# Turning more tiles on the matrix engine in a two-stage kernel's second half, with products two, three and four steps behind

## The chip, the cores and the metric

One core of a Trainium2 chip runs the whole program. Its engines work at the same time and wait for each other by semaphores: TensorE (PE in the profile, its weight loads PEld), VectorE (DVE), ScalarE (ACT), GpSimd (POOL), and SyncE (SP), which issues nearly all DMAs. Each engine takes its instructions strictly in the order in which the program lists them. The metric is the device time of one execution in microseconds (us); lower is better.

## The reference

An input of 8 x 3072 x 256 floats goes through three layers:

```
X  = rfft(x, axis=1);  Y = soft(X @ (w_r + i w_i) + b, 0.01)   # complex, soft-thresholded
x1 = irfft(Y)                                                # 24576 tokens of 256
logits = x1 @ phi                                            # 32 slots
d = softmax over tokens;  slot = d.T @ x1;  slot_out = relu(slot @ w1) @ w2   # per expert
c = softmax over slots;   x2 = c @ slot_out
h = x2 @ w_in                                                # 1024 wide
solu = h * softmax(h);  ln = (solu - mean) / sqrt(var + 1e-6) * g
out = ln @ w_out                                             # 24576 x 256
```

Only the last four lines concern the second half of the kernel. There `x2` is never formed: `slot_out @ w_in` is folded into one matrix `gst` of 128 x 1024, so that h comes from the 32 slot weights `c` of a token alone, and the mean is taken out of `w_out` beforehand (`gw`).

## The kernel before

The first half (`phase1`) computes the transform, the thresholded mix and the slot sums, batch by batch, and leaves the weights c in DRAM. A short middle part at the head of `phase2` (lines 858 to 933) computes the expert outputs, `gw` (the scaled and centred output weights as a rounded part `gw[:, :, 0]` and a remainder `gw[:, :, 1]`) and `gst`. The change touches this part lightly and the loop after it heavily.

The loop works on 192 tiles of 128 tokens (`NI`). What a tile goes through, with the helper's name:

- `hmat`: TensorE forms hps = -h (128 x 1024) from `ct` and `gst`, two matmuls into one of three PSUM buffers.
- `rowmax`: VectorE takes the row minimum of hps (the maximum of h); `expo`: ScalarE makes e = exp(h - max) and its row sum; `umul`: VectorE makes u = hps * e and its row sum. The hps buffer is free after `umul`.
- `blocks`: VectorE transposes u in 32 x 32 blocks (tile `tb`), and four DMAs gather the blocks into `t2`, which is u transposed.
- `uhi`: ScalarE (three quarters) and GpSimd (one quarter) round t2 into uh; `ulo`: GpSimd subtracts, ul = t2 - uh, in two halves of 512 columns.
- `prod`: TensorE multiplies by `gw` into `po2`: 16 matmuls of uh and then 8 of ul, of which the first four need the first half of ul and the last four the second.
- `vari`: ScalarE squares u and sums (`sq`); `rstd`: every fourth step, at step 3 modulo 4, GpSimd turns the sums of four tiles into scales, by four small instructions (tile `st`, lines 1138 to 1141); `outp`: ScalarE copies two products with their scales into `osb`; `store`: one DMA for four tiles.

A *turned* tile goes another way: `hmat` uses `gstn` (the same matrix in the natural column order), `turn` transposes u on TensorE by 8 matmuls into the tile's own hps buffer, ScalarE copies that out (`raw`), and GpSimd rounds and subtracts only half of it (`turned_parts`); its product has 4 fp32 matmuls with `gwf` (the unrounded weights) and 12 others. It has no `blocks` and no DMAs. Before, tiles 22, 30, 38, ... 182 are turned, 21 of them. The last two tiles (`direct`) also go through TensorE.

The order of the work is written out by hand in the loop's body, and each engine follows it. In step i (turn i of the loop) stand `hmat` of tile i+3, `rowmax` i+2, `umul` and `blocks` i+1, `vari` i, `expo` i+2, `uhi` and `ulo` i-2 with `rstd` between the two halves of `ulo`, and last `prod` i-4. Around a turned tile T, step T-1 ends with 16 matmuls of a product, the 8 transposes of tile T, and the 8 that are left; step T begins with 12 matmuls of the next product and then `hmat` of T+3, which waits for the copy of tile T's transposes, as it writes the same buffer. Every matmul has line 89 and every transpose line 92, since helpers record them.

## Time and profile before

| | us |
|---|---|
| median of three runs | 1342.22 (1339.57 to 1346.41) |
| the profiled execution, its own time | 1338.72 |
| its span, first to last instruction | 1336.8 |
| first `hmat` of the loop | 644.4 |
| busy over the span: PE, DVE, ACT, POOL | 1261.9, 1143.4, 982.2, 1013.6 |
| granted TensorE clock, mean | 0.982 |

The loop takes the second half of the span, from 644 on. In the profile a row of the timeline gives the start, the length, the engine, the source line, the operation, the output and input tiles, the shape, and in brackets how long the engine had stood idle before and what released it. A matmul's length there includes the pipeline's latency, so the cost of a group of matmuls is read from its start to the start of what follows. The granted clock is 1.00 at TensorE's full 2.4 GHz and 0.50 at the lower level of 1.2 GHz.

### The profile page before, as it was taken

The page shows a single profiled execution, that of the slowest core. Times are in us where ns is not written, and L with a number is a line of the kernel's source. Part 1 is how long each engine was busy: PE and PEld are TensorE (multiplying, and loading weights), DVE is VectorE, ACT ScalarE, POOL GpSimd, SP SyncE. Part 2 cuts the span into 40 slices and gives each one's busy share as a digit, 9 for nine tenths or more (in the row PEclk, how much of TensorE's full clock was granted, in tenths as well). Part 3 has the DMA queues.
Part 4 walks back from the last instruction along what each step waited for, and adds up shares of the span by engine and source line. Part 5 has one row for each costly group of instructions (what it writes and reads, how often), then busy time and mean ns, then how long its engine had stood idle before and what let it go on. Part 6 is the DMA issues. An engine that isn't in the chain of part 4 may idle for free.

```text
span 1336.8 us, 30801 instructions
## 1 busy us (share of the span) xinstructions
PE 1261.9 (94%) x10964; PEld 1110.8 (83%) x10964; DVE 1143.4 (86%) x1559; ACT 982.2 (73%) x1829; POOL 1013.6 (76%) x1115
## 2 busy tenths in 40 slices
PE   5989999999999999888599999999999999999998
PEld 2867878787878778864398999999999999999998
DVE  1858898887888988765798999999999999999993
ACT  3445556565555564443598999999999999999995
POOL 0869596867777675331299999998999989998896
PEclk8999999999999999998799999999999999999999
DMA  8987374655647283349477777777777777777763
GB/s 268 276 218 191 116 207 125 175 158 139 180 111 220 73 242 113 96 157 348 97 165 195 187 209 199 199 182 184 199 197 197 180 190 198 191 197 177 196 170 110
DMA packets 185961, 241.77 MB, mean 181 GB/s; under 512 B 21968, under 2 KB 145232, under 8 KB 185808
## 3 DMA queue, kind: packets, MB, share of 16 engines
q1 hardware_dynamic: 185472, 238.62, 66.3%
q8 instruction: 87, 1.43, 0.5%
q10 hardware_dynamic: 336, 1.18, 0.3%
q14 instruction: 66, 0.54, 0.1%
HBM read 92.00 MB, written 59.11 MB: 113 GB/s over the span
## 4 chain that ended last, share of the span: by engine, by line
PE 69%; POOL 10%; DVE 8%; DMA 5%; issue 4%; ACT 2%; SPq 1%; POOLq 0%; ACTq 0%; DVEq 0%
PE po L89 34%; PE pb L89 7%; PE pm L89 6%; PE hps L89 6%; PE xps L89 5%; PE s L89 4%; PE pa L89 3%; POOL ul L1094 3%; DMA xc<-in_x_dram 2%; PE sps L92 2%; POOL x L223 1%; POOL x L227 1%; PE hps L92 1%; POOL s L342 1%; DMA t<-tb 1%
## 5 line engine op out<-in xcount | busy, mean ns | idle before, releaser
L1094 POOL TENSOR_TENSOR ul<-t,uh 128x512 fp32r<-128x512 f32 x338 | 432.2, 1294 | 38.3 <-ACT uh L1080 38.1
L89 PEld LDWEIGHTS po<-gw,uh 128*128 128x128 f32 x2736 | 350.5, 190 | 14.0
L89 PE MATMUL po<-gw,uh 128*128 128x256 f32 x2736 | 356.8, 282 | 0.0
L984 DVE TENSOR_REDUCE st<-hps 128x1 f32<-128x1024 f32 x192 | 229.1, 1194 | 14.3 <-PE hps L89 14.3
L89 PE MATMUL po<-gw,ul 128*128 128x256 f32 x1620 | 230.4, 285 | 6.8 <-POOL ul L1094 6.6
L999 DVE SCALAR_TENSOR_TENSOR u<-hps,e 128x1024 f32<-128x1024 f32 x192 | 232.2, 1209 | 0.5 <-ACT e L991 0.5
L991 ACT ACTIVATE e<-hps,st 128x1024 f32<-128x1024 f32 x192 | 215.2, 1121 | 16.9 <-DVE st L984 16.9
L1104 ACT ACTIVATE sq<-u,st 128x1024 f32<-128x1024 f32 x192 | 222.9, 1161 | 0.2 <-DVE u L999 0.2
L1022 DVE STREAM_TRANSPOSE tb<-u 128x1024 f32<-128x1024 f32 x169 | 210.5, 1245 | 6.6 <-DMA t<-tb 0.7
L89 PEld LDWEIGHTS po<-gw,ul 128*128 128x128 f32 x1620 | 207.0, 189 | 9.3 <-POOL ul L1094 8.2
L342 POOL TENSOR_TENSOR s<-yb,s 128x512 f32<-128x512 f32 x95 | 124.4, 1309 | 112.3 <-DVE s L341 108.7
L89 PEld LDWEIGHTS xps<-d_sb,apt 128*128 128x128 f32 x768 | 95.1, 194 | 59.6 <-issue 35.6
L1080 ACT ACTIVATE uh<-t 128x768 fp32r<-128x768 f32 x169 | 143.4, 849 | 0.4 <-DMA t<-tb 0.4
L89 PE MATMUL xps<-d_sb,apt 128*128 128x128 f32 x768 | 111.2, 288 | 12.5 <-DMA apt<-ad 9.6
L89 PE MATMUL hps<-gst,ct 128*128 128x512 f32 x338 | 107.6, 401 | 14.3 <-DVE u L999 12.9
L250 ACT ACTIVATE asb<-s 128x1024 f32<-128x1024 f32 x56 | 57.3, 1024 | 85.4 <-PE s L89 74.2
L223 POOL TENSOR_TENSOR x<-xc 112x512 f32<-112x512 f32 x56 | 74.7, 1334 | 42.7 <-DMA xc<-in_x_dram 39.3
L307 POOL TENSOR_TENSOR sl<-xsum,sh 128x256 fp32r<-128x256 f32 x93 | 74.8, 804 | 35.4 <-ACT sh L306 35.1
L291 DVE TENSOR_TENSOR xsum<-xps,xi 128x256 f32<-128x256 f32 x96 | 39.7, 414 | 68.0 <-ACT xh L290 47.8
L1081 POOL CAST uh<-t 128x256 fp32r<-128x256 f32 x169 | 67.6, 400 | 39.1 <-DMA t<-tb 39.1
L1155 ACT ACTIVATE osb<-po,st 128x256 f32<-128x256 f32 x192 | 80.1, 475 | 11.4 <-PE po L89 11.4
L227 POOL TENSOR_TENSOR x<-xc 112x512 f32<-112x512 f32 x56 | 80.3, 1433 | 0.0
(204 smaller groups left out, 2354.8 us busy)
## 6 DMA issues: line engine op xcount, KB each, us to landing
t<-tb SPq DMA_DIRECT2D x676, 128.0 KB, 2.8
xc<-in_x_dram SPq DMA_DIRECT2D x128, 192.0 KB, 4.1
apt<-ad SPq DMA_DIRECT2D x96, 256.0 KB, 4.2
out_dram<-osb SPq DMA_DIRECT2D x47, 512.0 KB, 3.7
ad<-asb SPq DMA_DIRECT2D x112, 192.0 KB, 3.9
ct<-c_dram SPq DMA_DIRECT2D x96, 128.0 KB, 4.0
wt<-in_moe_w_dram SPq DMA_DIRECT2D x21, 512.0 KB, 9.5
ws<-in_moe_w_dram SPq DMA_DIRECT2D x22, 256.0 KB, 5.9
```

The lines of the kernel that those rows point to most:

```text
L89: PE.matmul(out=out, lhsT=lhsT, rhs=rhs, start=start, stop=stop)
L223: POOL.tensor_tensor(out=z[0:112, 0], in0=t[:, 0], in1=t[:, 1], op=ALU.add)
L227: POOL.tensor_tensor(out=z[0:112, 1], in0=t[:, 0], in1=t[:, 1], op=ALU.subtract)
L342: (DVE if last else POOL).tensor_tensor(out=s, in0=y, in1=s, op=ALU.subtract)
L984: DVE.tensor_reduce(out=st[:, 0, k:k + 1], in_=hps[i], op=ALU.min, axis=AX.X)
L991: ACT.activation(out=e, in_=hps[i], func=AF.Exp, bias=st[:, 0, k:k + 1], scale=-1.0, accum_out=st[:, 1, k:k + 1])
L999: DVE.scalar_tensor_tensor(out=u, in0=hps[i] if turned(i) else hps.pop(i), scalar=1.0, in1=et.pop(i), op0=ALU.mult, op1=ALU.mult, accum_ou ...
L1022: DVE.transpose(out=t, in_=ut[i])
L1080: ACT.activation(out=w[:, 0:HA], in_=v[:, 0:HA], func=AF.Copy)
L1094: POOL.tensor_tensor(out=ul[:, z, :].rearrange("p c (a j) -> p c a j", a=4), in0=v, in1=w.bitcast(F32), op=ALU.subtract)
L1104: ACT.activation(out=sq, in_=ut.pop(i), func=AF.Square, bias=st[:, 2, k:k + 1], scale=-float(DFF), accum_out=st[:, 3, k:k + 1])
L1155: ACT.activation(out=o[:, k], in_=pot.pop(i), func=AF.Copy, scale=stt[j][:, 4, k:k + 1])
```

## The change

In the loop, five more tiles are turned (6, 10, 14, 18 and 26), so that up to 30 it is every fourth one, 26 in all. `prod` runs L steps behind, 2 for steps below 64, 3 below 128, then 4; at steps 64 and 128 one step has no product. `uhi` and `ulo` take tile i-1 in steps up to 95, none in step 96, and tile i-2 from step 97. `outp` runs as soon as both products of a pair are L+2 steps old or more (by the counter `pair`), and a store follows two steps after. In the first steps 24 matmuls of `ones` on `ones` go to a spare PSUM buffer (`run_on`). In the middle part the centring of `wo`, the rounding and the remainder are done in two halves, the first of which leaves its result in `gwf`; `gstn` is copied as `gst` is made; three h1 buffers serve h1 and h1t.

```
--- before.py
+++ after.py
@@ -835,6 +835,8 @@
         gw = k_p.tile([128, 8, 2, D], F32R, name="gw")
         gw_h, gw_l = gw[:, :, 0, :], gw[:, :, 1, :]
         gst = k_p.tile([128, DFF], F32R, name="gst")
+        gstn = k_p.tile([128, DFF], F32R, name="gstn")
+        gwf = k_p.tile([128, 4, D], F32, name="gwf")
         cts = {}
 
 
@@ -862,8 +864,10 @@
         load_c(0, 0)
         load_ws(len(ws_todo))
         wo = gw_t["wo"]
-        DVE.tensor_tensor(out=wo, in0=wo, in1=gm.to_broadcast([128, 8, D]), op=ALU.subtract)
-        ACT.activation(out=gw_h, in_=wo, func=AF.Copy)
+        g_halves = ((slice(0, 4), gwf), (slice(4, 8), wo[:, 4:8]))
+        for z, o in g_halves:
+            DVE.tensor_tensor(out=o, in0=wo[:, z], in1=gm.to_broadcast([128, 4, D]), op=ALU.subtract)
+            ACT.activation(out=gw_h[:, z], in_=o, func=AF.Copy)
 
 
         so = t_p.tile([128, 2, D], F32, name="so")
@@ -880,14 +884,14 @@
                             dh == 0,
                             dh == 1,
                         )
-            h1 = t_p.tile([128, DFF], F32, name="h1", tag="h1", bufs=2)
+            h1 = t_p.tile([128, DFF], F32, name="h1", tag="h1", bufs=3)
             ACT.activation(out=h1[:, 0:512], in_=ph[0], func=AF.Relu)
             DVE.tensor_scalar(out=h1[:, 512:1024], in0=ph[1], scalar1=0.0, scalar2=None, op0=ALU.max)
             h1s[eh] = h1
         load_c(0, 1)
         load_c(0, 2)
         for eh in range(2):
-            h1t = t_p.tile([128, 8, 128], F32, name="h1t", tag="h1t", bufs=2)
+            h1t = t_p.tile([128, 8, 128], F32, name="h1t", tag="h1", bufs=3)
             for k in range(2):
                 pst = pt.tile([128, 4, 128], F32, name="pst", tag="pt")
                 for j in range(4):
@@ -897,7 +901,8 @@
                 else:
                     ACT.activation(out=h1t[:, 4 * k:4 * k + 4, :], in_=pst, func=AF.Copy)
             h1ts[eh] = h1t
-        DVE.tensor_tensor(out=gw_l, in0=wo, in1=gw_h.bitcast(F32), op=ALU.subtract)
+        for z, o in g_halves:
+            DVE.tensor_tensor(out=gw_l[:, z], in0=o, in1=gw_h[:, z].bitcast(F32), op=ALU.subtract)
 
         wi_h = g_p.tile([128, 2, DFF], F32R, name="wi_h", tag="wo")
         for dh in range(2):
@@ -931,15 +936,15 @@
             v = pg[fh].rearrange("p (c j b) -> p b c j", c=4, b=4)
             ACT.activation(out=o, in_=v, func=AF.Copy)
             DVE.tensor_tensor(out=o[64:128], in0=v[64:128], in1=o[64:128].bitcast(F32), op=ALU.subtract)
+            POOL.tensor_copy(
+                out=gstn[:, 512 * fh:512 * fh + 512].rearrange("p (c j b) -> p b c j", c=4, b=4), in_=o.bitcast(F32)
+            )
         p.close()
         pw.close()
 
         def right(name, bufs, **k):
             return p2.enter_context(tc.tile_pool(name=name, bufs=bufs, side="right", **k))
 
-        f_p = right("f_p", 1)
-        gwf = f_p.tile([128, 8, D], F32, name="gwf")
-        gstn = f_p.tile([128, DFF], F32R, name="gstn")
         e_p = right("e_p", 2)
         u_p = right("u_p", 4)
         o_p = right("o_p", 2)
@@ -1004,16 +1009,7 @@
             return i >= NI - 2
 
         def turned(i):
-            return i % 8 == 6 and 16 < i < NI - 2
-
-        def gst_order():
-            POOL.tensor_copy(out=gstn.rearrange("p (c j b) -> p b c j", c=8, b=4), in_=gst.rearrange("p (b c j) -> p b c j", b=4, c=8).bitcast(F32))
-
-
-
-        def gw_sum(n):
-            z = slice(2 * n, 2 * n + 2)
-            POOL.tensor_tensor(out=gwf[:, z], in0=gw[:, z, 0].bitcast(F32), in1=gw[:, z, 1].bitcast(F32), op=ALU.add)
+            return i >= 6 and i % (4 if i < 32 else 8) == 2 + 4 * (i >= 32) and i < NI - 2
 
         def blocks(i):
             if i >= NI or direct(i) or turned(i):
@@ -1157,7 +1153,7 @@
 
                 SP.dma_start(out=v[:, k, :], in_=o[:, k, :])
             elif k == 3:
-                o_todo[i + 2] = (v, o)
+                o_todo[i] = (v, o)
 
 
         def store(i):
@@ -1194,27 +1190,40 @@
         pieces(1)
         for i in range(3):
             hmat(i)
+        idle = po_p.tile([128, 128], F32, name="idle", tag="po2")
+
+        def run_on():
+            for _ in range(8):
+                mm(idle, ones, ones)
+
+        run_on()
         rowmax(0)
         expo(0)
         rowmax(1)
         expo(1)
         umul(0)
         blocks(0)
+        pair = 0
         for i in range(NI + 6):
             j, k = divmod(i, 4)
+            L = 2 if i < 64 else 3 if i < 128 else 4
             if turned(i):
-                prod(i - 4, 12)
+                prod(i - L, 12)
             hmat(i + 3)
+            if i < 2:
+                run_on()
             trans(i)
             rowmax(i + 2)
             umul(i + 1)
             blocks(i + 1)
-            store(i - 6)
+            for t in [t for t in o_todo if t + L + 4 <= i]:
+                store(t)
             late_c(i)
             last_c(i)
-            if i % 2 == 1:
-                outp(i - 7)
-                outp(i - 6)
+            if 2 * pair + 3 + L <= i:
+                outp(2 * pair)
+                outp(2 * pair + 1)
+                pair += 1
             if turned(i):
                 expo(i + 2)
                 vari(i)
@@ -1222,22 +1231,19 @@
                 vari(i)
                 expo(i + 2)
             direct_parts(i)
-            if i <= NI + 1:
-                uhi(i - 2)
-                ulo(i - 2, 0)
+            m = i - (1 if i < 96 else 2)
+            if i != 96 and 0 <= m < NI:
+                uhi(m)
+                ulo(m, 0)
             rstd(i)
-            if i <= NI + 1:
-                ulo(i - 2, 1)
-            if i == 8:
-                gst_order()
-            if i in (10, 12, 14, 16):
-                gw_sum(i // 2 - 5)
+            if i != 96 and 0 <= m < NI:
+                ulo(m, 1)
             if k == 1:
                 pieces(j + 2)
             if turned(i + 1):
-                prod(i - 4, 8)
+                prod(i - L, 8)
                 turn(i + 1)
-            prod(i - 4)
+            prod(i - L)
         while o_todo:
             store(min(o_todo))
 
```

The first place is TensorE's start of the loop, from the second hps on: hps are the `hmat` products, po2 the products of uh and ul. Before:

```order
L89 MATMUL hps_8654<-gst_8355,ct_8386 128x512 x2
L89 MATMUL hps_8671<-gst_8355,ct_8386 128x512 x2
L89 MATMUL hps_8695<-gst_8355,ct_8386 128x512 x2
L89 MATMUL hps_8722<-gst_8355,ct_8386 128x512 x2
L89 MATMUL po2_8745<-gw_8354,uh_8689 128x256 x16
L89 MATMUL po2_8745<-gw_8354,ul_8690 128x256 x8
L89 MATMUL hps_8770<-gst_8355,ct_8442 128x512 x2
L89 MATMUL po2_8745<-gw_8354,uh_8712 128x256 x16
L89 MATMUL po2_8745<-gw_8354,ul_8713 128x256 x8
```

And now:

```order
L89 MATMUL hps_8617<-gst_8355,ct_8388 128x512 x2
L89 MATMUL hps_8620<-gst_8355,ct_8388 128x512 x2
L89 MATMUL idle_8623<-ones_64 128x128 x8
L89 MATMUL hps_8648<-gst_8355,ct_8388 128x512 x2
L89 MATMUL idle_8623<-ones_64 128x128 x8
L89 MATMUL hps_8673<-gst_8355,ct_8388 128x512 x2
L89 MATMUL idle_8623<-ones_64 128x128 x8
L89 MATMUL hps_8704<-gst_8355,ct_8388 128x512 x2
L89 MATMUL po2_8728<-gw_8354,uh_8698 128x256 x16
L89 MATMUL po2_8728<-gw_8354,ul_8699 128x256 x8
```

The first product stands two hps earlier, and the three groups of idle matmuls stand ahead of the fourth to sixth hps.

The second place is TensorE from the hps of tile 38 (of `gstn`, as the tile is turned) on, in steps 35 to 37. Before, the low part that `rstd` of step 35 cuts in two is ul_10316, of tile 33:

```order
L89 MATMUL hps_10294<-gstn_8591,ct_9290 128x512 x2
L89 MATMUL po2_10277<-gw_8354,uh_10223 128x256 x16
L89 MATMUL po2_10277<-gw_8354,ul_10224 128x256 x8
L89 MATMUL hps_10349<-gst_8355,ct_9290 128x512 x2
L89 MATMUL po2_10372<-gw_8354,uh_10271 128x256 x16
L89 MATMUL po2_10372<-gw_8354,ul_10272 128x256 x8
L89 MATMUL hps_10397<-gst_8355,ct_9705 128x512 x2
L89 MATMUL po2_10372<-gw_8354,uh_10315 128x256 x16
L92 MATMUL hps_10294<-ident_62,u_10401 128x128 x8
L89 MATMUL po2_10372<-gw_8354,ul_10316 128x256 x8
```

Now it is ul_10355, of tile 34:

```order
L89 MATMUL hps_10335<-gstn_8356,ct_9359 128x512 x2
L89 MATMUL po2_10310<-gw_8354,uh_10304 128x256 x16
L89 MATMUL po2_10310<-gw_8354,ul_10305 128x256 x8
L89 MATMUL hps_10388<-gst_8355,ct_9359 128x512 x2
L89 MATMUL po2_10411<-gw_8354,uh_10354 128x256 x16
L89 MATMUL po2_10411<-gw_8354,ul_10355 128x256 x8
L89 MATMUL hps_10436<-gst_8355,ct_9753 128x512 x2
L89 MATMUL po2_10411<-gw_8354,uh_10405 128x256 x16
L92 MATMUL hps_10335<-ident_62,u_10440 128x128 x8
```

From the hps of tile 38 to this low part there were two more hps, and now there is one.

The third place is around step 103, after turned tile 102. On GpSimd the low part of tile 101 (ul_13718 before, ul_13724 now) is cut in two by `rstd`. Before:

```order
L1081 CAST uh_13717<-t2_13549 128x256
L1094 TENSOR_TENSOR ul_13718<-t2_13549,uh_13717 128x512
L1138 TENSOR_SCALAR st_13448<-st_13448 128x4
L1139 TENSOR_TENSOR st_13448<-st_13448 128x4
L1140 TENSOR_TENSOR st_13448<-st_13448 128x4
L1141 TENSOR_TENSOR st_13448<-st_13448,mhalf_8610 128x4
L1094 TENSOR_TENSOR ul_13718<-t2_13549,uh_13717 128x512
```

And now, in the same order:

```order
L1077 CAST uh_13723<-t2_13556 128x256
L1090 TENSOR_TENSOR ul_13724<-t2_13556,uh_13723 128x512
L1134 TENSOR_SCALAR st_13447<-st_13447 128x4
L1135 TENSOR_TENSOR st_13447<-st_13447 128x4
L1136 TENSOR_TENSOR st_13447<-st_13447 128x4
L1137 TENSOR_TENSOR st_13447<-st_13447,mhalf_8612 128x4
L1090 TENSOR_TENSOR ul_13724<-t2_13556,uh_13723 128x512
```

On TensorE before, from the hps of step 102 to the product of tile 101:

```order
L89 MATMUL hps_13655<-gst_8355,ct_12907 128x512 x2
L89 MATMUL po2_13642<-gw_8354,uh_13558 128x256 x4
L89 MATMUL po2_13642<-gw_8354,ul_13559 128x256 x8
L89 MATMUL hps_13691<-gst_8355,ct_12907 128x512 x2
L89 MATMUL po2_13642<-gw_8354,uh_13601 128x256 x16
L89 MATMUL po2_13642<-gw_8354,ul_13602 128x256 x8
L89 MATMUL hps_13751<-gst_8355,ct_12907 128x512 x2
L89 MATMUL po2_13770<-gw_8354,uh_13673 128x256 x16
L89 MATMUL po2_13770<-gw_8354,ul_13674 128x256 x8
L89 MATMUL hps_13795<-gst_8355,ct_12907 128x512 x2
L89 MATMUL po2_13770<-gw_8354,uh_13717 128x256 x16
L89 MATMUL po2_13770<-gw_8354,ul_13718 128x256 x8
```

And now:

```order
L89 MATMUL hps_13661<-gst_8355,ct_12922 128x512 x2
L89 MATMUL po2_13613<-gw_8354,uh_13607 128x256 x4
L89 MATMUL po2_13613<-gw_8354,ul_13608 128x256 x8
L89 MATMUL hps_13701<-gst_8355,ct_12922 128x512 x2
L89 MATMUL po2_13733<-gw_8354,uh_13683 128x256 x16
L89 MATMUL po2_13733<-gw_8354,ul_13684 128x256 x8
L89 MATMUL hps_13758<-gst_8355,ct_12922 128x512 x2
L89 MATMUL po2_13733<-gw_8354,uh_13723 128x256 x16
L89 MATMUL po2_13733<-gw_8354,ul_13724 128x256 x8
```

GpSimd's order is unchanged there; on TensorE the product of tile 101 stands one step earlier, after the second hps that follows and not after the third.

## Rows read from the trace of the kernel before

**Rows 1.** Windows: stretch, us, busy (count) of PE, PEld, DVE, ACT, POOL, clock, DMA, GB/s.

```profile
716.50:719.70 3.20, 3.20 (x18) 3.15 (x17) 3.18 (x4) 3.20 (x6) 3.20 (x5) 0.56 0.88 209
...
732.80:760.37 27.57, 27.57 (x215) 26.62 (x213) 26.67 (x31) 26.99 (x49) 26.60 (x36) 1.00 0.80 203
760.37:789.78 29.41, 28.20 (x214) 26.85 (x213) 27.20 (x32) 27.02 (x50) 28.60 (x37) 1.00 0.82 215
...
844.98:872.58 27.60, 27.60 (x214) 26.65 (x213) 26.89 (x32) 27.02 (x49) 25.14 (x32) 1.00 0.75 191
```

**Rows 2.** Waits of VectorE from 775 to 1310: who, total us, times, longest.

```profile
DVE st L984 <- PE hps L89: 10.6, 20, 1.9
```

**Rows 3.** Timeline of all engines, the period of turned tile 54.

```profile
841.67 1.09 PE L92 MATMUL hps<-ident,u 128*128 128x128 f32 x8
...
844.98 0.62 PE L89 MATMUL hps<-gst,ct 128*128 128x512 f32 x2
...
845.64 1.22 DVE L984 TENSOR_REDUCE st<-hps 128x1 f32<-128x1024 f32 x1 [0.47 <-PE hps L89]
...
850.16 0.62 PE L89 MATMUL hps<-gst,ct 128*128 128x512 f32 x2
...
850.60 1.30 POOL L1094 TENSOR_TENSOR ul<-t,uh 128x512 fp32r<-128x512 f32 x1 [0.78 <-ACT uh L1080]
...
852.50 1.10 PE L89 MATMUL po<-gw,ul 128*128 128x256 f32 x8
...
853.44 0.62 PE L89 MATMUL hps<-gst,ct 128*128 128x512 f32 x2
...
853.79 1.30 POOL L1094 TENSOR_TENSOR ul<-t,uh 128x512 fp32r<-128x512 f32 x1
...
859.81 1.19 DVE L984 TENSOR_REDUCE st<-hps 128x1 f32<-128x1024 f32 x1
...
863.20 1.30 POOL L1094 TENSOR_TENSOR ul<-t,uh 128x512 fp32r<-128x512 f32 x1 [0.17 <-ACT uh L1080]
...
865.97 1.11 PE L89 MATMUL po<-gw,ul 128*128 128x256 f32 x8
866.39 1.30 POOL L1094 TENSOR_TENSOR ul<-t,uh 128x512 fp32r<-128x512 f32 x1
...
869.14 0.08 DVE L999 DVE_READ_ACCUMULATOR u<-hps,e 128x1 f32 x1
...
869.27 1.09 PE L92 MATMUL hps<-ident,u 128*128 128x128 f32 x8
```

**Rows 4.** Timeline, start of the loop and the hps of tile 33.

```profile
645.19 2.36 DVE L984 TENSOR_REDUCE st<-hps 128x1 f32<-128x1024 f32 x2 [0.83 <-PE hps L89]
...
655.50 0.40 POOL L1081 CAST uh<-t 128x256 fp32r<-128x256 f32 x1 [39.08 <-DMA t<-tb]
...
656.19 1.19 PE L89 MATMUL hps<-gst,ct 128*128 128x512 f32 x2 [2.34 <-DVE u L999]
...
664.25 2.12 PE L89 MATMUL po<-gw,uh 128*128 128x256 f32 x9
...
760.37 0.62 PE L89 MATMUL hps<-gst,ct 128*128 128x512 f32 x2
```

**Rows 5.** Timeline of TensorE, its waits for GpSimd between 697 and 774.

```profile
699.37 0.74 PE L89 MATMUL po<-gw,ul 128*128 128x256 f32 x4 [1.29 <-POOL ul L1094]
...
715.20 0.75 PE L89 MATMUL po<-gw,ul 128*128 128x256 f32 x4 [2.06 <-POOL ul L1094]
...
716.55 3.29 PE L89 MATMUL po<-gw,uh 128*128 128x256 f32 x16
...
773.42 0.75 PE L89 MATMUL po<-gw,ul 128*128 128x256 f32 x4 [1.21 <-POOL ul L1094]
```

**Rows 6.** Timeline of TensorE, fp32 matmuls of 128 columns; the last weights.

```profile
520.65 0.61 PE L89 MATMUL xps<-d_sb,apt 128*128 128x128 f32 x4
...
637.07 1.05 PE L89 MATMUL po<-ws,h1t 128*32 128x256 f32 x10 [0.54 <-DMA ws<-in_moe_w_dram]
```

More of the change, by code (lines that the diff above doesn't have):

```diff
@@ L837, in phase2 @@
         gst = k_p.tile([128, DFF], F32R, name="gst")
+        gstn = k_p.tile([128, DFF], F32R, name="gstn")
+        gwf = k_p.tile([128, 4, D], F32, name="gwf")
         cts = {}
@@ L864, in phase2 @@
         wo = gw_t["wo"]
-        DVE.tensor_tensor(out=wo, in0=wo, in1=gm.to_broadcast([128, 8, D]), op=ALU.subtract)
-        ACT.activation(out=gw_h, in_=wo, func=AF.Copy)
+        g_halves = ((slice(0, 4), gwf), (slice(4, 8), wo[:, 4:8]))
+        for z, o in g_halves:
+            DVE.tensor_tensor(out=o, in0=wo[:, z], in1=gm.to_broadcast([128, 4, D]), op=ALU.subtract)
+            ACT.activation(out=gw_h[:, z], in_=o, func=AF.Copy)
         so = t_p.tile([128, 2, D], F32, name="so")
@@ L882, in phase2 @@
                         )
-            h1 = t_p.tile([128, DFF], F32, name="h1", tag="h1", bufs=2)
+            h1 = t_p.tile([128, DFF], F32, name="h1", tag="h1", bufs=3)
             ACT.activation(out=h1[:, 0:512], in_=ph[0], func=AF.Relu)
@@ L889, in phase2 @@
         for eh in range(2):
-            h1t = t_p.tile([128, 8, 128], F32, name="h1t", tag="h1t", bufs=2)
+            h1t = t_p.tile([128, 8, 128], F32, name="h1t", tag="h1", bufs=3)
             for k in range(2):
@@ L899, in phase2 @@
             h1ts[eh] = h1t
-        DVE.tensor_tensor(out=gw_l, in0=wo, in1=gw_h.bitcast(F32), op=ALU.subtract)
+        for z, o in g_halves:
+            DVE.tensor_tensor(out=gw_l[:, z], in0=o, in1=gw_h[:, z].bitcast(F32), op=ALU.subtract)
         wi_h = g_p.tile([128, 2, DFF], F32R, name="wi_h", tag="wo")
@@ L933, in phase2 @@
             DVE.tensor_tensor(out=o[64:128], in0=v[64:128], in1=o[64:128].bitcast(F32), op=ALU.subtract)
+            POOL.tensor_copy(
+                out=gstn[:, 512 * fh:512 * fh + 512].rearrange("p (c j b) -> p b c j", c=4, b=4), in_=o.bitcast(F32)
+            )
         p.close()
@@ L938, in right @@
             return p2.enter_context(tc.tile_pool(name=name, bufs=bufs, side="right", **k))
-        f_p = right("f_p", 1)
-        gwf = f_p.tile([128, 8, D], F32, name="gwf")
-        gstn = f_p.tile([128, DFF], F32R, name="gstn")
         e_p = right("e_p", 2)
@@ L1006, in turned @@
         def turned(i):
-            return i % 8 == 6 and 16 < i < NI - 2
-        def gst_order():
-            POOL.tensor_copy(out=gstn.rearrange("p (c j b) -> p b c j", c=8, b=4), in_=gst.rearrange("p (b c j) -> p b c j", b=4, c=8).bitcast(F32))
-        def gw_sum(n):
-            z = slice(2 * n, 2 * n + 2)
-            POOL.tensor_tensor(out=gwf[:, z], in0=gw[:, z, 0].bitcast(F32), in1=gw[:, z, 1].bitcast(F32), op=ALU.add)
+            return i >= 6 and i % (4 if i < 32 else 8) == 2 + 4 * (i >= 32) and i < NI - 2
         def blocks(i):
@@ L1196, in phase2, with run_on @@
             hmat(i)
+        idle = po_p.tile([128, 128], F32, name="idle", tag="po2")
+        def run_on():
+            for _ in range(8):
+                mm(idle, ones, ones)
+        run_on()
         rowmax(0)
@@ L1202, in phase2 @@
         blocks(0)
+        pair = 0
         for i in range(NI + 6):
             j, k = divmod(i, 4)
+            L = 2 if i < 64 else 3 if i < 128 else 4
             if turned(i):
-                prod(i - 4, 12)
+                prod(i - L, 12)
             hmat(i + 3)
+            if i < 2:
+                run_on()
             trans(i)
@@ L1211, in phase2 @@
             blocks(i + 1)
-            store(i - 6)
+            for t in [t for t in o_todo if t + L + 4 <= i]:
+                store(t)
             late_c(i)
             last_c(i)
-            if i % 2 == 1:
-                outp(i - 7)
-                outp(i - 6)
+            if 2 * pair + 3 + L <= i:
+                outp(2 * pair)
+                outp(2 * pair + 1)
+                pair += 1
             if turned(i):
@@ L1224, in phase2 @@
             direct_parts(i)
-            if i <= NI + 1:
-                uhi(i - 2)
-                ulo(i - 2, 0)
+            m = i - (1 if i < 96 else 2)
+            if i != 96 and 0 <= m < NI:
+                uhi(m)
+                ulo(m, 0)
             rstd(i)
-            if i <= NI + 1:
-                ulo(i - 2, 1)
-            if i == 8:
-                gst_order()
-            if i in (10, 12, 14, 16):
-                gw_sum(i // 2 - 5)
+            if i != 96 and 0 <= m < NI:
+                ulo(m, 1)
             if k == 1:
@@ L1237, in phase2 @@
             if turned(i + 1):
-                prod(i - 4, 8)
+                prod(i - L, 8)
                 turn(i + 1)
-            prod(i - 4)
+            prod(i - L)
         while o_todo:
```

2 lines of the change are left out of this document (1 added, 1 removed).

## Prediction

> **What bounds the kernel now.** I read the table of windows first, then the waits, then the timeline of one whole period; only the second half is touched. Below, step i is turn i of the loop over the 192 tiles, and T is a turned tile. From tile 22 on the second half repeats every 8 tiles, from the first hps product of step T to that of step T+8: 27.57, once 29.41, and then 27.60 us each time, with TensorE busy for all of it and VectorE for 26.89 [rows 1]. That reads as bound by TensorE. The waits say it less simply: VectorE waited for hps 20 times between 775 and 1310, 10.6 us in all [rows 2], about once a period.
>
> The timeline shows what closes the loop [rows 3]. This is the period of T=54. The hps product of tile T+3 starts at 844.98, and VectorE, which had waited 0.47, takes its minimum at 845.64. From there VectorE runs without a gap at 3.54 a step (859.81 less 845.64, over 4 steps) until the u of tile T+8 ends at 869.22. TensorE's transposes of that u start at 869.27, 0.05 later. Then come the rest of a product, 12 matmuls of the next and the next hps product; the same stretch one period earlier runs from 841.67 to 844.98, 3.31 us. So the loop hps, seven VectorE steps, transposes, hps takes 27.6 us by itself, and TensorE's own work (8 steps of 3.28, that is 853.44 less 850.16, and 1.36 more for a turned tile) takes 27.6 as well. Neither has room, and a saving on TensorE alone shortens no such period.
>
> Before tile 22 it is VectorE that never stops: 33 steps of 3.54 from its first minimum at 645.19 would end near 762, and the hps of tile 33 starts at 760.37 [rows 4].
>
> **The change part by part. The start.** Products begin at step 2 instead of 4. TensorE's first product now starts at 664.25, while the hps of step 2 starts at 656.19 [rows 4]; the new one should start near 656.7, so 7.5 us of idling go. Against this stand five more turned tiles (6, 10, 14, 18 and 26; 22 and 30 were turned before): 5 x 1.36 = 6.8 us on TensorE, 5 x 1.2 less on VectorE (27.6 less the wait of 0.47 and seven steps of 3.54 leave 2.35 for the step of a turned tile). What counts is when the hps of tile 33 (T=30) starts. TensorE has now to do, from 656.2, 28 steps (2 to 29) at 3.28 = 91.8, six turned tiles at 1.36 = 8.2, and the stretch of 3.31 ahead of that hps less the eight matmuls that any step has (about 1), 2.3. That ends at 758.5 without a wait. I add 3.0 us of waits: 2.1 at tile 2, where four small statistics instructions stand on GpSimd between the two halves of the low part (the pattern worked out below), and 0.9 for the two first products, which follow GpSimd's splits at once. So 761.5, against 760.37: **+1.1**. TensorE, at about 14.5 for four tiles, is now behind VectorE (3 x 3.54 + 2.4 = 13.0), and the time that VectorE is spared there is spent waiting. Bounds: -2 with no wait, +3 with the first two products at the lower clock (1.4 each, worked out below).
>
> **The other edits of the start.** The 24 idle matmuls stand in waits of TensorE; eight fp32 ones of about this shape take about 1.2 (four took 0.61) [rows 6], some 2.4 at the lower clock, and the wait ahead of the hps at 656.19 is 2.34 [rows 4]: cost 0, at most 0.3. The halved gw subtraction, the shared h1 buffers and gwf, written where the subtraction already passes, stand before 637, where TensorE waits for the ws weights in any case [rows 6]: 0, within 0.5 either way. The two gstn copies fall on GpSimd, idle for 39.08 us until 655.50 [rows 4]: 0. That GpSimd no longer makes gstn and gwf between tiles 8 and 16 takes away waits like those at 715.20 (2.06) [rows 5], but VectorE set the pace there, so nothing is credited.
>
> **The period of 29.41.** 1.81 above the rule, with a wait of 1.21 for GpSimd at 773.42 [rows 5]; GpSimd is busy for 28.60 of it, 26.60 of the one before and 25.14 later [rows 1], because it splits the last batch's c in steps 24 to 30. This loss goes (**-1.8**), but the same c work now falls among turned tiles with products only two steps behind: I put **+1.5**, between 0 and 3.
>
> **Products two steps behind, steps 32 to 63.** Every fourth step GpSimd does four statistics instructions between the halves of the low part: first half from 863.20, second from 866.39 to 867.69. What it splits there now is tile T+4, one later than before, and TensorE uses it one step later instead of two. In the rows TensorE comes to the eight low matmuls of that step at 865.97; the last four need the second half and would start half of 0.95 later, at 866.44. They must wait until 867.69: 1.25 us. GpSimd's chain starts at VectorE's minimum at 845.64, which itself follows TensorE's hps, so the wait returns each period and lengthens it to 28.85. Tiles 34, 42, 50, 58: 4 x 1.25 = **+5.0**.
>
> **Splits a step later, products three behind, steps 97 to 127.** The order is again one step between split and use. Now tile T-1 is the one cut in two by the statistics: its halves run from 850.60 and from 853.79 to 855.09. TensorE reaches the low matmuls of that step at 852.50, their second half at 852.97: a wait of 2.12 us, after which the later wait of the same period is covered. Tiles 101, 109 and 117: 3 x 2.12, and tile 97 as above 1.25: **+7.6**. For the waits of both stages together the bounds are 0, if the splits come earlier than in these rows, and 12.6 and the clock (below).
>
> **The steps at 64 and 128**, where TensorE leaves out one product of 2.8 us: it comes to the next transposes early and finds u not ready, by the 0.05 us above. Gain 0, bounds 0 and 2.8 each. Stores follow the output copies by two steps as before: 0.
>
> **Sum.** 1338.7 (the profiled execution's own time, with a span of 1336.8) + 1.1 + 1.5 - 1.8 + 5.0 + 7.6 = 1352.1. That execution was 3.5 us below the median of the three runs, which by itself would put the sum at 1355.6. I forecast **1352 us**, as waits worked out this way can only turn out smaller where an engine runs ahead of the rows.
>
> **Rivals.** *The start pays.* If TensorE alone set the pace, the 7.5 us at the start, the waits of 1.29, 2.06 and 1.21 for GpSimd [rows 5] and 1.4 of lower clock after the second would all be saved, less 6.8 for the turned tiles and 0.9 for two hps products that now come after the first product: 1338.7 - 7.5 - 4.6 - 1.4 + 6.8 + 0.9, about 1333. For it: TensorE is busy in 27.60 of 27.60. Against it: the 0.05 us between u and the transposes. Chance 0.08.
>
> *Nothing is late.* The start gives nothing and the waits for GpSimd do not come: 1338.7 + 0.8, about 1340. For it: GpSimd has 2.5 us free in each period. Against it: that room lies elsewhere than between these two halves. Chance 0.22.
>
> *The clock falls too.* After the wait of 2.06 at 715.20 the granted clock was 0.56 from 716.5 to 719.7 (the lower level, 1.2 GHz, for most of it), and 16 matmuls took 3.29, as long as a whole step at the full clock [rows 1, 5]: 3.2 x 0.44, 1.4 us lost. In the period that holds the wait of 1.21 the clock stayed at 1.00 [rows 1]. Three waits of 2.12 would cost 1.4 more each, 1356, and two first products at the lower clock 3 more: 1359. It decides if waits of 2 us recur in every period. Chance 0.13. [...]
>
> **How the numbers follow.** The forecast, 1345 to 1356, has 0.57, the clock 0.13, nothing late 0.22, the start 0.08. A difference of 0.5%, 6.7 us, is about what can be told from no change here. Nearly all of the forecast and all of the clock's case lie beyond it, nothing late inside it; the start, at 5.8 below, is just inside it, and half of its chance is counted beyond: faster 0.05, same 0.26, slower 0.69. The range goes from 1338 to 1361; it takes in nothing late and the clock, and leaves out the start and a clock that falls more often.
>
> **What would show it.** In the new profile: TensorE waiting for ul four times by 1.2 between tiles 34 and 58 and three times by 2.1 near tiles 101, 109 and 117; periods of 28.9 and 29.7 there and 27.6 elsewhere from tile 62 on; the hps of tile 33 near 761; transposes 0.05 behind u in the periods after steps 64 and 128. I am wrong if the hps of tile 33 starts before 756, if a period of eight tiles is shorter than 27.5, or if TensorE never waits for ul after tile 33.

## The result and the profile after

The changed kernel takes 1357.61 us (median of 4 runs, 1354.45 to 1358.45) against 1341.16 for the kernel before in the same session (4 runs, 1339.57 to 1346.41): ratio 1.0118, 95% interval 1.0092 to 1.0144. It is slower by 16.5 us; the forecast was 1352, or 13.4 more than the profiled execution before. The profiled execution took 1357.04, 18.3 more than that of before.

Windows of the profile after, each from the transposes of a turned tile to those of the next (columns as in [rows 1], whose period of 27.60 they answer to): tile 26 to 30, 30 to 38, 38 to 46, 46 to 54, 70 to 78, 110 to 118.

```profile
743.58:758.23 14.65, 14.65 (x110) 13.95 (x109) 13.13 (x17) 13.83 (x25) 14.16 (x20) 1.00 0.68 165
758.23:789.96 31.73, 29.80 (x214) 28.29 (x213) 27.35 (x32) 27.18 (x49) 27.58 (x35) 0.95 0.74 193
789.96:821.52 31.56, 29.66 (x214) 28.19 (x214) 27.70 (x34) 27.31 (x49) 26.55 (x33) 0.95 0.70 186
821.52:851.03 29.51, 27.82 (x215) 26.73 (x214) 26.16 (x30) 27.25 (x48) 23.60 (x30) 1.00 0.66 164
...
907.60:935.17 27.57, 27.57 (x213) 26.58 (x213) 26.89 (x32) 27.47 (x51) 25.93 (x32) 1.00 0.75 192
...
1048.92:1078.67 29.75, 28.25 (x215) 26.63 (x214) 27.10 (x32) 27.09 (x48) 25.19 (x32) 1.00 0.70 178
```

The loss stands in two blocks: tiles 30 to 62 and 94 to 126. Between and behind them a period is 27.5 to 27.6 as before. In the long periods no engine is busy all the time. What VectorE waits for shows it too; the wait from 775 to 1310 that answers to [rows 2]:

```profile
DVE st L989 <- PE hps L89: 23.9, 24, 2.7
```

The start of the loop in the timeline of TensorE (it answers to [rows 4]): first hps, first product, the wait at tile 2 and what follows it, the hps of tile 33.

```profile
642.85 1.67 PE L89 MATMUL hps<-gst,ct 128*128 128x512 f32 x6 [1.42 <-DVE gst L938]
...
655.35 2.15 PE L89 MATMUL po<-gw,uh 128*128 128x256 f32 x16
...
667.00 1.16 PE L89 MATMUL po<-gw,ul 128*128 128x256 f32 x4 [1.91 <-POOL ul L1090]
667.96 1.05 PE L89 MATMUL hps<-gst,ct 128*128 128x512 f32 x2
...
761.48 0.62 PE L89 MATMUL hps<-gst,ct 128*128 128x512 f32 x2
```

The hps at 667.96 takes 1.05 where one at the full clock takes 0.62: the clock fell after the wait.

The first block, in the timeline of all engines: the end of the period from tile 30 and of the one from tile 38.

```profile
781.33 0.20 POOL L1134 TENSOR_SCALAR st<-st 128x4 f32<-128x4 f32 x1
...
782.16 1.01 POOL L1137 TENSOR_TENSOR st<-st,mhalf 128x4 f32<-128x4 f32 x1
...
783.14 1.26 POOL L1090 TENSOR_TENSOR ul<-t,uh 128x512 fp32r<-128x512 f32 x1
...
784.46 0.74 PE L89 MATMUL po<-gw,ul 128*128 128x256 f32 x4 [1.13 <-POOL ul L1090]
...
785.56 0.84 ACT L1076 ACTIVATE uh<-t 128x768 fp32r<-128x768 f32 x1 [3.28 <-DMA t<-tb]
...
786.45 3.68 PE L89 MATMUL po<-gw,uh 128*128 128x256 f32 x16 [0.80 <-ACT uh L1076]
...
817.05 1.05 PE L89 MATMUL po<-gw,ul 128*128 128x256 f32 x4 [1.90 <-POOL ul L1090]
...
818.75 2.93 PE L89 MATMUL po<-gw,uh 128*128 128x256 f32 x16
```

The four statistics instructions (L1134 to L1137) end at 783.17; the second half of ul follows and ends at 784.40, and TensorE waits for it. Two things were not in the sum of the forecast. The next tile's transfer t<-tb reached ScalarE 3.28 late, and its product waited again. And the 16 matmuls behind these waits took 3.68, and 2.93 in the next period, where 2.04 is the rule.

The second block, one period of it:

```profile
1054.80 1.94 PEld L89 LDWEIGHTS po<-gw,uh 128*128 128x128 f32 x16 [0.61 <-ACT uh L1076]
1054.80 2.15 PE L89 MATMUL po<-gw,uh 128*128 128x256 f32 x16 [0.17 <-ACT uh L1076]
...
1057.43 0.53 PEld L89 LDWEIGHTS po<-gw,ul 128*128 128x128 f32 x4 [0.21 <-POOL ul L1090]
...
1060.98 1.28 POOL L1090 TENSOR_TENSOR ul<-t,uh 128x512 fp32r<-128x512 f32 x1
...
1062.31 0.53 PEld L89 LDWEIGHTS po<-gw,ul 128*128 128x128 f32 x4 [1.51 <-POOL ul L1090]
```

### The profile page after: what moved, and what is told of

Read it like the earlier page. It is cut to its first block, busy times and chain, and to the rows that moved or that the text cites. A ratio compares the mean times of both kernels' runs of the same rounds, so it can differ in the third digit from the quotient of the medians.

```text
span 1355.3 us, 30893 instructions
## 1 busy us (share of the span) xinstructions
PE 1277.3 (94%) x11032; PEld 1122.0 (83%) x11032; DVE 1140.1 (84%) x1556; ACT 984.3 (73%) x1830; POOL 1005.2 (74%) x1107
## 4 chain that ended last, share of the span: by engine, by line
PE 51%; DVE 13%; POOL 11%; DMA 9%; issue 7%; ACT 5%; SPq 4%; DVEq 0%; POOLq 0%; ACTq 0%
PE po L89 18%; PE pb L89 7%; PE pm L89 6%; POOL ul L1090 5%; PE xps L89 5%; DMA t<-tb 4%; PE s L89 4%; DVE u L1004 3%; PE pa L89 3%; PE hps L89 3%; SPq L1022 3%; DMA xc<-in_x_dram 2%; DVE st L989 2%; DVE tb L1018 2%; PE sps L92 2%
## 5 line engine op out<-in xcount | busy, mean ns | idle before, releaser
L1090 POOL TENSOR_TENSOR ul<-t,uh 128x512 fp32r<-128x512 f32 x328 | 419.4, 1297 | 63.9 <-ACT uh L1076 61.1
L89 PEld LDWEIGHTS po<-gw,uh 128*128 128x128 f32 x2656 | 340.4, 190 | 17.4 <-ACT uh L1076 4.5
L89 PE MATMUL po<-gw,uh 128*128 128x256 f32 x2656 | 348.1, 282 | 1.5 <-ACT uh L1076 1.3
L89 PE MATMUL po<-gw,ul 128*128 128x256 f32 x1640 | 238.1, 287 | 15.5 <-POOL ul L1090 15.5
L89 PEld LDWEIGHTS po<-gw,ul 128*128 128x128 f32 x1640 | 211.0, 189 | 20.8 <-POOL ul L1090 19.1
L1018 DVE STREAM_TRANSPOSE tb<-u 128x1024 f32<-128x1024 f32 x164 | 204.3, 1246 | 5.7
L1076 ACT ACTIVATE uh<-t 128x768 fp32r<-128x768 f32 x164 | 140.1, 854 | 6.7 <-DMA t<-tb 6.5
L89 PE MATMUL xps<-d_sb,apt 128*128 128x128 f32 x768 | 110.9, 288 | 11.9 <-DMA apt<-ad 9.0
L89 PE MATMUL hps<-gst,ct 128*128 128x512 f32 x328 | 103.1, 397 | 5.9 <-DVE u L1004 4.5
```

What stands on the lines that cost most here:

```text
L89: PE.matmul(out=out, lhsT=lhsT, rhs=rhs, start=start, stop=stop)
L1018: DVE.transpose(out=t, in_=ut[i])
L1076: ACT.activation(out=w[:, 0:HA], in_=v[:, 0:HA], func=AF.Copy)
L1090: POOL.tensor_tensor(out=ul[:, z, :].rearrange("p c (a j) -> p c a j", a=4), in0=v, in1=w.bitcast(F32), op=ALU.subtract)
```

## The experiments

The theory: between split and product there is one step where there were two, and the four statistics instructions on GpSimd don't fit into one. The rival: one step is too little by itself, because of the transfers or of ScalarE's copies. Unless said otherwise each kernel is the changed one with the edit shown. All ratios are to the kernel before, on the same chip. The first hps comes anywhere from 642.9 to 651.7 in these profiles, by what the first half of the kernel does, which no edit touches (the changed kernel was 1.54 early at its matmul pm<-ft_sb at 597 already), so the table counts from there. Each row is one profiled execution. In the code, `...` marks lines left out; where m is changed, the step without a split goes or moves with it.

| kernel | tr. 30 | 30 to 62 | 94 to 126 | tr. 182 | ratio (95% interval) |
|---|---|---|---|---|---|
| before | 112.7 | 112.2 | 110.4 | 638.9 | 1 |
| changed | 115.4 | 121.9 | 118.1 | 658.6 | 1.0118 (1.0092 to 1.0144) |
| e1_split_early | 115.4 | 118.1 | 110.4 | 650.4 | 1.0064 (1.0042 to 1.0086) |
| e2_stats_behind | 113.1 | 116.3 | 112.1 | 646.0 | 1.0042 (1.0024 to 1.0060) |
| e3_lag_from32 | 113.8 | 111.4 | 110.3 | 638.9 | 1.0012 (0.9991 to 1.0033) |
| e4_lag_in_dense | 110.1 | 110.6 | 110.4 | 634.6 | 0.9981 (0.9961 to 1.0002) |
| e5_thirds | 109.7 | 111.3 | 110.4 | 635.0 | 0.9969 (0.9953 to 0.9985) |
| e6_c_store_late | 115.4 | 117.5 | 118.1 | 655.5 | 1.0120 (1.0095 to 1.0145) |
| e7_three_behind | 114.1 | 121.8 | 110.4 | 649.8 | 1.0047 (1.0031 to 1.0063) |
| e8_four_behind | 111.5 | 110.9 | 110.4 | 636.3 | 0.9990 (0.9975 to 1.0005) |
| e9_thirds_c_late | 109.0 | 111.1 | 110.4 | 634.2 | 0.9978 (0.9961 to 0.9995) |
| e10_no_idle | 113.8 | 119.0 | 118.1 | 654.2 | 1.0123 (1.0097 to 1.0149) |
| e11_no_statistics | 112.2 | 114.3 | 112.1 | 642.0 | 1.0013 (0.9995 to 1.0032) |

Columns: us from the first hps to the transposes of tile 30; from those of tile 30 to those of 62; from 94 to 126; from the first hps to the transposes of tile 182.

**e1_split_early**

```
-            m = i - (1 if i < 96 else 2)
+            m = i - 1
...
```

> The changed kernel with the splits one step after the tile all the way (no shift at step 96); products three and four behind stay. Theory (the wait is the statistics between the two halves of ul, and counts only where the product follows the split by one step): the periods of 29.75 from tile 102 to 126 and the 28.82 before them become 27.6, 7.7 us less than the changed kernel, about 1350; the periods 30 to 62 stay at 31.7, 31.6, 29.5 and 29.1. Rival (in those steps the split is late for another reason, the transfers or ScalarE, so that its step doesn't matter): 1357, periods of 29.7 stay.

1350.55: the periods from tile 94 to 126 are back at 27.6, 7.7 less. The theory held there. Two things were not expected. The first block, in whose steps this kernel has the changed kernel's code, took 118.1 and not 121.9: here the granted clock stayed at 1.00 in the two periods where the changed kernel's profile has 0.95, so some 3 of the 9.7 us by which that profile exceeds the kernel before in this block are the lower clock, which comes in one profile and not in the other with the same code. The windows from tiles 30 and 38:

```profile
767.09:796.93 29.84, 28.29 (x215) 26.78 (x214) 26.77 (x31) 25.69 (x47) 26.65 (x34) 1.00 0.75 198
796.93:826.44 29.51, 28.24 (x214) 26.69 (x213) 27.46 (x32) 28.61 (x51) 25.84 (x33) 1.00 0.75 190
```

And behind tile 134 five periods became 27.9 to 28.5. GpSimd and ScalarE wait for t<-tb there; GpSimd's waits from 1135 to 1300 (us in all, times, longest):

```profile
POOL uh L1077 <- DMA t<-tb: 5.4, 5, 2.5
```

**e2_stats_behind**

```
-            rstd(i)
             if i != 96 and 0 <= m < NI:
                 ulo(m, 1)
+            rstd(i)
```

> The changed kernel with the four statistics instructions behind the second half of ul instead of between the halves; all else as it is. Theory: the second half then ends about 1.8 earlier, every wait for ul but a remainder of 0.3 goes, periods from tile 46 on come down to 27.6 to 28, and the two half-clock stretches with them: 1340 to 1346. Rival (the transfers t<-tb reach ScalarE and GpSimd too late for a product one step behind the split, whatever the order on GpSimd): the periods 30 to 54 stay above 30 and those of 29.75 fall by half at most, 1350 or more.

1345.26: in the first block 116.3, 5.6 less than in the changed kernel but only 1.8 less than in e1, where the clock also stayed at 1.00; in the second, 6 of the 7.7 us gone. That is between the two. Part of the price only changed its place. In the timeline of all engines, from the period of tile 54 on, the output copy osb now waits for the statistics on ScalarE, the next e is late, and VectorE's u after it:

```profile
872.51 0.84 ACT L1151 ACTIVATE osb<-po,st 128x256 f32<-128x256 f32 x2 [1.64 <-POOL st L1137]
...
875.61 1.23 DVE L1004 SCALAR_TENSOR_TENSOR u<-hps,e 128x1024 f32<-128x1024 f32 x1 [1.55 <-ACT e L996]
```

**e3_lag_from32**

```
-            L = 2 if i < 64 else 3 if i < 128 else 4
+            L = 2 if i < 32 else 4
...
-            m = i - (1 if i < 96 else 2)
+            m = i - (1 if i < 32 else 2)
...
```

> The changed kernel with only its first 32 steps two behind; from step 32 on products four behind and splits two behind, as in the kernel before. Theory (all of the loss lies in the steps where a product follows its split by one): transposes of tile 30 near 758, then periods of 27.6 throughout, 1340 to 1342, within 0.2% of the kernel before, the two products left out at step 32 giving nothing. Rival (the many turned tiles of the start leave ScalarE, GpSimd or the transfers behind, and this is paid after tile 30): 1346 or more, with the period 30 to 38 still above 30.

1341.66, as the theory said: with the lag of before from step 32 on the loss is gone. Two products less at step 32 gave nothing: that period takes 28.69, where e8_four_behind, with no product left out there, takes 27.84. Its window shows TensorE idle for 3.7 us, at a lower mean clock:

```profile
761.10:789.79 28.69, 25.02 (x166) 22.84 (x165) 26.76 (x32) 25.75 (x46) 24.16 (x31) 0.88 0.76 201
```

**e4_lag_in_dense**

```
+            L = 2 if i < 8 else 3 if i < 18 else 4
+            m = i - (1 if i < 18 else 2)
```

(in place of the lines for L and m; the step without a split is 18)

> The changed kernel with the products let fall back inside the stretch of every fourth tile (two behind to step 8, three to step 18, four from there, splits two behind from step 18), as in the kernel before afterwards. Theory: in that stretch TensorE, at 14.45 for four tiles, is the only limit, and the loop through VectorE needs 13.3 (u is ready 1.1 before its transposes), so up to 5 of the 5.6 us of two products left out are gained: transposes of tile 30 near 753, then 27.6 a period, 1335 to 1337, faster than both kernels. Rival (another engine, GpSimd with 12 to 14 busy of 14.4, sets that pace as well): transposes of tile 30 at 757 or later, 1340.

1339.34, not told apart from the kernel before. The direction was right (tile 30 is 5.3 earlier than in the changed kernel), but the loop through VectorE binds just where the expectation had put it, near 13.3: a period of 14.44 can give only 1.1 that way, so the 5 us did not follow. Windows of its periods from tiles 6, 10, 18 and 22: the products left out gave 1.07 and 2.25, not 2.8 each. The second gave more because 12 of its matmuls stand in that loop, between the transposes and the next hps: without them the hps comes 1.82 after the transposes (714.45 to 716.27) instead of 3.22 (672.36 to 675.58).

```profile
672.36:685.73 13.37, 11.94 (x86) 10.86 (x85) 11.64 (x15) 12.19 (x21) 10.97 (x15) 1.00 0.47 109
685.73:700.13 14.40, 14.40 (x108) 13.85 (x109) 13.85 (x16) 13.49 (x25) 11.83 (x16) 1.00 0.75 188
714.45:726.64 12.19, 11.40 (x91) 10.75 (x89) 11.97 (x16) 11.46 (x22) 7.63 (x11) 1.00 0.69 176
726.64:741.03 14.39, 14.39 (x109) 13.85 (x110) 13.62 (x16) 14.39 (x27) 12.92 (x18) 1.00 0.73 181
```

**e5_thirds**

```
+            N = min(max(i - 2, 0) // 4, 6)
+            L = 2 + -(-N // 3)
+            P = 24 * (i - 1) - 24 // 3 * N
...
-            prod(i - L)
+            upto(P)
...
```

(upto runs the products to a position in 24ths of a tile; splits two behind from step 18; statistics behind ul for the first four tiles)

> As e4_lag_in_dense, but the two products fall back by a third at each of the turned tiles 6, 10, 14, 18, 22 and 26, and the statistics of the first four tiles stand behind the second half of ul. Theory (a period of four tiles can't be shorter than the 13.37 that e4 shows once, the loop through VectorE, so a whole product dropped at once gains 1.07 to 2.2 of its 2.8, and a third dropped each time nearly all of its 0.93): six periods near 13.5, transposes of tile 30 some 108 after the first hps against 112.7 of the kernel before and 110.1 of e4; 1334 to 1336, 0.4% to 0.5% below the kernel before. Rival (another limit than TensorE's and VectorE's holds the dense stretch near 14): no better than e4, 1338 to 1339.

1336.90: faster than the kernel before, by 0.15% to 0.47%, and than the changed one. The window from tile 26 has the 13.4, but the transposes of tile 30 come 109.7 after the first hps, not 108, and the time is 0.9 above the range of the theory: in the periods from tiles 18 and 22 TensorE waits for ul, the first time here. (That no period can be shorter than 13.37 holds for the loop with those 12 matmuls in it; e4's 12.19 stands beside it.) Whether the thirds help is not shown: from the first hps to tile 182 this kernel takes 635.0, and e4, with whole products, 634.6.

```profile
742.64:756.04 13.40, 13.40 (x103) 12.84 (x101) 12.08 (x16) 13.02 (x23) 12.92 (x18) 1.00 0.70 186
```

```profile
726.23 0.75 PE L89 MATMUL po<-gw,ul 128*128 128x256 f32 x4 [1.07 <-POOL ul L1090]
```

**e6_c_store_late**

```
-            elif i == 33:
+            elif i == 73:
```

> The changed kernel with the two stores of the last batch's c issued at step 73 instead of 33. Theory (they stand ahead of the transfers t<-tb on SP, and with one step between split and product ScalarE's wait of 3.28 for t<-tb reaches TensorE): the period of 31.7 from tile 30 falls to 29 or 30, the later ones stay at 29 to 31.5, the periods of 29.75 stay: 1354 to 1356. Rival (that transfer is late without them too): the wait of about 3 stays, 1357.

In the trace the theory held for the wait: the period from tile 30 is 29.18 and ScalarE's long wait for t<-tb is gone (0.16 is left at that place). So the stores of c ahead of the transfers had made it. What the wait costs is less than 31.73 less 29.18, since the clock stayed at 1.00 here: in e1 and e10, with the stores at step 33 and the clock at 1.00, ScalarE waits 2.9 and 2.6 and the period is 29.84 and 30.39, so 0.7 to 1.2. At step 73 the stores cost 1.1 again (the period from tile 78 is 28.73).

```profile
760.54:789.72 29.18, 27.99 (x215) 26.83 (x213) 27.16 (x32) 27.31 (x49) 27.23 (x35) 1.00 0.72 184
```

From tile 30 to 182 it needs 3.0 less than the changed kernel, about what the lower clock took there, so moving the stores gained nothing that can be told apart. The time, 1357.00, is the rival's number; its interval is 3.4 to either side.

**e7_three_behind**

```
+            L = 2 if i < 64 else 3
...
+            m = i - 1
...
```

> The changed kernel with products three behind from step 64 to the end and splits one behind throughout. Theory (two steps between split and product are enough; what e1_split_early lost after step 128 came from products four and splits one behind, which needs a fifth uh buffer for as long as it has): 27.6 in every period from tile 62 on, 3 below e1_split_early, 1347 to 1349. Rival (splits one behind are late for other reasons after step 128 too): 28.4 a period there, 1350 or more.

1346.67, 0.3 below the range of the theory: 27.5 or 27.6 in every period from tile 62 on. Two steps between split and product are enough here. What e1 lost behind tile 134 came with products four behind; that the uh buffers are what is short there was not tried by itself. Its first block, which has no edit, again shows the lower clock:

```profile
759.55:790.80 31.25, 29.58 (x214) 28.10 (x213) 27.20 (x32) 26.99 (x48) 27.54 (x35) 0.95 0.76 197
790.80:822.84 32.04, 30.14 (x213) 28.29 (x213) 27.74 (x33) 27.42 (x49) 26.60 (x33) 0.94 0.70 183
```

**e8_four_behind**

```
+            L = 4
...
+            m = i - 2
...
```

> The changed kernel with products four and splits two behind throughout, as in the kernel before: what is left of the change is the turned tiles 6 to 26, the edits of the start and the idle matmuls. Theory: TensorE, which starts its products at step 4 again, needs 26 steps of 3.28, six times 1.36 and 3.7 besides, so transposes of tile 30 come about 113.8 after the first hps (112.7 in the kernel before), then 27.6 a period, without the 29.4: 1339 to 1342, the same as the kernel before. Rival (the turned tiles relieve VectorE and the start is won): 1335 or less.

1339.53, the same as the kernel before. Five more turned tiles with the old lag cost nothing: the transposes of tile 30 come 111.5 after the first hps, 1.2 earlier than before and 2.3 earlier than the theory had them, and the period from tile 30 is 27.84 instead of 29.4.

**e9_thirds_c_late**

```
-            elif i in (24, 26, 28, 30):
+            elif i in range(33, 65, 4):
...
-            elif i == 33:
+            elif i == 70:
```

(on top of e5; the pieces of c are half as long; splits fall back at step 20)

> As e5_thirds, with the splits falling back at step 20 instead of 18 and the split of the last batch's c in eight pieces at steps 33 to 61 (stores at 70) instead of four at 24 to 30. Theory (what e5 still lost, 15.1 and 14.0 a period from tiles 18 and 22 and 28.6 from tile 30, are waits of 1.1, 1.2 and 0.5 for GpSimd, late by the shifted split and by the c work): every dense period at 13.4 to 13.7, transposes of tile 30 some 107 after the first hps (109.7 in e5), 27.6 to 27.9 from there, 2 to 3 below e5, 1333 to 1335, 0.5% below the kernel before. Rival (those waits only move to the c work's new place, eight waits of 0.5 or so): as e5, 1337.

1338.65: not told apart from e5 (their intervals overlap), though tile 182 is reached 0.8 earlier from the first hps. The theory's 2 to 3 us are not there; the period from tile 22 stays at 13.99 and the one from tile 30 at 28.32.

**e10_no_idle**

```
         def run_on():
+            return
```

> The changed kernel without its 24 idle matmuls. Theory (they keep the clock up for the first products): the 16 high matmuls of tiles 0 and 1 take 3.6 and 2.9 or so instead of 2.15 and 2.06, and as TensorE is the limit from there to tile 30, its transposes come 2 later than in the changed kernel (115.4 after the first hps), about 1359.5. Rival (a first product that starts 7 earlier has its slack): 1357.5, the same.

The rival held: 1357.08. The first products do run at the lower clock, as expected, and it costs nothing here, because the wait for the second half of ul at tile 2 shrinks from 1.91 to 0.30 (timeline of TensorE):

```profile
659.22 3.62 PE L89 MATMUL po<-gw,uh 128*128 128x256 f32 x16
662.64 1.58 PE L89 MATMUL po<-gw,ul 128*128 128x256 f32 x8
...
670.64 0.73 PE L89 MATMUL po<-gw,ul 128*128 128x256 f32 x4 [0.30 <-POOL ul L1090]
```

**e11_no_statistics**

```
         def rstd(i):
-            if i >= NI:
+            if i < NI - 4 or i >= NI:
...
```

> The changed kernel without the four statistics instructions of the tiles up to 187 (their outputs are scaled by a constant instead). Theory (these 2.1 us of GpSimd, every fourth step, are what products one step behind their splits can't bear): no wait for ul over 0.5 but in the c stores' period, 27.6 in every other period from tile 38, 27.6 to 30 from tile 30: 1339 to 1343. Rival (one step between split and product is too little by itself, by the transfers t<-tb or ScalarE's copies): periods of 28.5 or more stay between tiles 38 and 62 and 102 and 126, 1347 or more.

1342.18: the statistics are most of it. From tile 38 to 62 the periods are 28.0, 27.6 and 27.8, where e1 has 29.5, 29.5 and 29.2. But the rival has its part. The period from tile 30 stays at 31.0: ScalarE waits 2.56 for t<-tb behind the stores of c, TensorE 1.76 for ScalarE, and the 16 matmuls behind that wait take 3.67 instead of 2.04, as the clock fell (0.95 in this period). And the periods from tile 102 to 126 keep 0.55 each; TensorE's weight load waits up to 0.61 for ScalarE's uh in them, its matmuls less. Timeline of the first, and waits of TensorE's matmuls from 1009 to 1122:

```profile
784.73 3.67 PE L89 MATMUL po<-gw,uh 128*128 128x256 f32 x16 [1.76 <-ACT uh L1076]
```

```profile
PE po L89 <- ACT uh L1076: 0.7, 4, 0.2
```

## Why the prediction was right, and where it was not

The direction, the mechanism of the waits and the two places were right. The number was 5.5 short: 1357.61 lies above the forecast's own 1345 to 1356, and inside the whole range for the room that was left to the rival with the lower clock. In the profile, the lower clock is indeed most of what the sum left out.

**What bounds the kernel.** The loop hps, seven VectorE steps, transposes was right. At steps 64 and 128, where TensorE has one product less, a period of 27.51 stands for 27.60: TensorE comes early and waits for u (timeline after, the transposes of tile 70). e3, which leaves out two products at step 32, gains nothing either, though the clock fell there too.

```profile
907.60 1.09 PE L92 MATMUL hps<-ident,u 128*128 128x128 f32 x8 [0.89 <-DVE u L1004]
```

The four-tile form of the same loop, 13.4 with the 12 matmuls in it, is what held back e4.

**The start.** The sum gave 761.5 for the hps of tile 33; it came at 761.48. That is partly luck: counted from the first hps the changed kernel needs 118.6 and the kernel before 116.0, so the term is +2.7 and not +1.1; the first half was 1.57 early. The difference is the clock behind the wait at tile 2. In three of six profiles with that wait (changed, e1, e6) the clock fell behind it and the transposes of tile 6 come 28.6 after the first hps, in the others (e3, e4, e7) 27.1. The wait itself was sized well, 2.1 for 1.91. The 0.9 for waits of the two first products did not come: there is no wait for GpSimd ahead of the one at tile 2. The bound of +3 for first products at the lower clock was too wide: e10 has them, and they cost nothing.

**The other edits of the start:** 0, as far as the idle matmuls go, by e10; the rest was not tried by itself.

**Tiles 30 to 62.** Here the forecast fell short. It had 112.2 - 1.8 + 1.5 + 5.0 = 116.9; the changed kernel needs 121.9, e7 121.8, and e1 and e10, with the same code in these steps, 118.1 and 119.0. The largest part is the lower clock, which was in no term of the sum: 0.95 in two periods of 31.6, which costs 3.2 us, of these four in the changed kernel and e7 only. The rival "the clock falls too" had its mechanism right and its place wrong: it expected the clock to fall at tiles 101 to 117, where it stayed at 1.00. That its 1356 to 1359 comes nearest to the measured time is therefore partly luck.

The other part is the wait. It was taken as 1.25 each time from [rows 3], and is 1.13, 1.90, 1.69 and 1.26 in the changed kernel. In e10 and e1, with the clock at 1.00, the three periods from tile 38 take 29.3 to 29.8 and 29.2 to 29.5 where 28.85 was forecast: longer, and not shorter, as the forecast had argued for waits worked out this way. In [rows 3] GpSimd starts the first half after a wait of 0.17 for ScalarE's uh; now this wait is 0.79 ahead of the longer wait of TensorE below, but it is 0.78 ahead of the one of 1.13 too, so that does not settle why the waits differ.

```profile
843.60 1.30 POOL L1090 TENSOR_TENSOR ul<-t,uh 128x512 fp32r<-128x512 f32 x1 [0.79 <-ACT uh L1076]
...
848.11 0.74 PE L89 MATMUL po<-gw,ul 128*128 128x256 f32 x4 [1.69 <-POOL ul L1090]
```

The -1.8 is right (27.84 in e8). The 1.5 for the work on c has the right size, partly by luck: the period from tile 30 is 29.84 and 30.39 in e1 and e10, 1.0 and 1.5 above 28.85. But the term counted GpSimd alone, and 0.7 to 1.2 of it are the two stores of c on SP, which delay t<-tb (e6). I had costed the stores that follow the output copies at 0 and never looked at the other stores in that queue.

**Tiles 97 to 127.** 3 x 2.12 and 1.25 were forecast; 3 x 2.15 and 1.22 came, and e1 took away 7.7. The 2.12 is right for a somewhat wrong reason: TensorE's weight load waits 1.51 for the second half, not 2.12, and the other 0.6 go with small waits earlier in the period, 0.61 for ScalarE's uh and 0.21 for GpSimd's ul; e11, without the statistics, keeps 0.55.

**The rivals.** "Nothing is late" and "the start pays" are out: TensorE waits for ul in every period of both blocks, and the start costs 2.7 in the profile, and 1.1 to 1.4 in those of e3, e7 and e10, instead of gaining.

The sum of the misses: 1.6 at the start and 5.0 in tiles 30 to 62, less 1.6 of the first half, is 5.0 for the 4.9 us by which the profile exceeds the sum. Of those 6.6 us of misses, the lower clock is about 4.7 (1.5 at tile 2, 3.2 in the first block), all of it read from one execution; how often the clock falls there in the changed kernel's others is not on record.

## What to carry to other kernels

Shortening the distance between a producer and its consumer can pay only if the engine that waited sets the pace; here two loops of equal length set it, and the slack that was taken away came back as waits. Before a distance is cut by a step, look at the longest chain that can stand within that step on every engine and queue between the two, rare work included (here every fourth step's statistics, and two stores that are issued once). And a lag that must grow back is better given back where TensorE alone sets the pace, here among the first tiles: e4, e5 and e9 do so and reach tile 182 in 634.2 to 635.0 instead of 638.9. Of these, e5 and e9, a third of a product at a time, are faster than the kernel before by more than their intervals; that thirds are better than whole products is not shown, as the times of e4 and e5 overlap.
